# A gate's x*sigmoid(x) as one ScalarE function, and a visit's two exponentials as one instruction

## The chip, the core and the metric

The kernel runs on one core of one Trainium2 chip. A core has five engines that run side by side, each through its own list of instructions, in order: TensorE (PE in the rows, with its weight loads as PEld), VectorE (DVE), ScalarE (ACT), GpSimd (POOL) and SyncE (SP), which here only issues DMAs. They wait for one another through semaphores. TensorE writes its products to PSUM, which has eight banks of 128 x 512 numbers. The metric is the device time of one execution in microseconds (us).

## What is computed

Attention over 8 batches, 8 heads, 576 positions and 64 numbers per head, with a mask that leaves each position 32 earlier ones, next to each other for the first four heads and four apart for the last four; then a gated layer on the 4608 x 512 result.

```python
def _attn_ref(q, k, v):
    scores = scale * np.matmul(q, k.transpose(0, 1, 3, 2))
    ...
    scores = np.where(masks[None, :, :, :], scores, -1000000000.0)
    scores = scores - np.max(scores, axis=-1, keepdims=True)
    attn = np.exp(scores)
    attn = attn / (np.sum(attn, axis=-1, keepdims=True) + 1e-09)
    return np.matmul(attn, v).astype(np.float32)

def _moe_ref(x, w_gate, w_val, w_out):
    g = x @ w_gate
    silu = g * (1.0 / (1.0 + np.exp(-g)))
    val = x @ w_val
    return (silu * val @ w_out).astype(np.float32)
```

w_gate and w_val are 512 x 1536, w_out is 1536 x 512, all float32.

## The kernel before

Every float32 factor of the gated layer is split into a high and a low part, and a product is three matmuls (high by high, low by high, high by low).

The attention is cut into packs of tokens. The first four packs are done in an opening stage. Each later pack m has two **visits**, A and B, that are placed between the matmuls of the gated layer by the table `visit`: 31 packs are handled so (4 to 34). Visit A of a pack does, on TensorE, the result products of the pack before (L522) and its own scores (L459), both in the bank pair `two`; then VectorE normalizes the former (L530 to L532) and takes mask, maximum and difference of the latter (L477, or L472 for pack 4, then L479 and L480), and ScalarE takes the exponentials in `far_exps`. These are two instructions over the same 128 x 512 numbers, once to `s` (L492) and once in place to `e` (L487 in `exps`). Four DMAs (L497) then exchange quarters between the two, and VectorE transposes at visit B (L511).

The **plain stage** runs the gated layer on the first three chunks of 512 tokens, in 36 steps s (12 slices f of the 1536 columns for each chunk). A step is 12 matmuls into bank `bg` (gate, L587), 12 into `bv` (value, L587) and 12 output matmuls of the step before (L636). Each of `bg` and `bv` is one bank. So the gate matmuls of step s+1 wait until the readers of step s are done with `bg`: `act_tanh` on ScalarE, which writes t = tanh(g/2) to SBUF (L608), and `dve_u` on VectorE, which computes (t+1)*g from `bg` (L613). `dve_h` then multiplies by 0.5 and by `bv` (L618), and the result is split by ScalarE (L623) and GpSimd (L628).

During the first chunk the weights are still coming in as 64-bit integers. A unit u (half a slice f) is turned into its two parts by steps on three engines: ScalarE L253 and, for some units, L270; VectorE L273 and L283, or L280 alone; ScalarE L290 (high part); GpSimd L294 (low part). Units 0 and 1 are done in pieces, the rest as 128 x 768. Step s needs units 2s and 2s+1, and the conversion runs about one step ahead.

The **mixed stage** does the other three chunks (of 1024 tokens) with seven products of half-size blocks in place of eight. `keep` (L939, ScalarE) copies a bank that the next products go on adding to; `total` (L895, VectorE) adds bank and copy; `gated` applies tanh (L960) and the two VectorE steps (L962, L963) to these sums in SBUF; `h_split` splits the result (L924, L895).

The opening stage stands in an order written out by hand. After it a scheduler orders the instructions of each engine by its own estimates, kept by dependences and by the `behind(...)` marks. Tanh and Exp run from one table of ScalarE, which is loaded once at the start (L678).

Of the kernel before, what the change touches and what calls it, by code (L numbers as in the profile page):

```python
# [15 lines left out]
AF = mybir.ActivationFunctionType  # L16
ALU = mybir.AluOpType

P = 128
D = 64  # L20
# [121 lines left out]
def attention_moe(ctx, tc, qkb, vb, w, masks, ident, out):  # L142
# [201 lines left out]
    early, later = {}, {}  # L344
    for k, n in (("qk", QKB), ("v", NG * NH * (D + 1)), ("e", TP), ("pt", TP)):
        later[k] = Ring(n, o)
        o += n
# [96 lines left out]
    def scores(m, two, masked):  # L444
# [9 lines left out]
        for j in range(NH):  # L454
            for g in range(NG):
                q, k = BQ * (NH * g + j), FQN + pk(m).kcol[g, j] + o
                for h in range(2):
# [3 lines left out]
                                     stop=not masked or j == NH - 1, skip_group_check=True)  # L461

    def shift(m, two, pool, masked):

        mx, s, e = pool["bm"](2 * NH), pool["pt"](TP), pool["e"](TP)
        w = BK - 1 + masked
# [18 lines left out]
    def exps(m):  # L485
        e = st[m]["e"]
        last["e"] = nc.scalar.activation(out=e, in_=e, func=AF.Exp, scale=0.125)  # L487

    def far_exps(m):

        e, s = st[m]["e"], st[m]["s"]
        nc.scalar.activation(out=s, in_=e, func=AF.Exp, scale=0.125)  # L492
        exps(m)
        for g in range(0, NG, 2):
# [110 lines left out]

    def act_tanh(i):
        t = t_ring()
        last["t"] = nc.scalar.activation(out=t, in_=bank_g[:, :CH], func=AF.Tanh, scale=0.5)  # L608
        hst[i] = [t, None, None]

    def dve_u(i):
        t = hst[i][0]
        last["h"] = nc.vector.scalar_tensor_tensor(out=t, in0=t, scalar=1.0, in1=bank_g[:, :CH],  # L613
                                                   op0=ALU.add, op1=ALU.mult)

    def dve_h(i):
        t = hst[i][0]
        last["h"] = nc.vector.scalar_tensor_tensor(out=t, in0=t, scalar=0.5, in1=bank_v[:, :CH],  # L618
                                                   op0=ALU.mult, op1=ALU.mult)

# [333 lines left out]
    def gated(i, t):  # L954
# [4 lines left out]
        f = f_ring()  # L959
        nc.scalar.activation(out=f, in_=g, func=AF.Tanh, scale=0.5)  # L960
        v = total(t, 1, v_ring)
        nc.vector.scalar_tensor_tensor(out=f, in0=f, scalar=1.0, in1=g, op0=ALU.add, op1=ALU.mult)  # L962
        nc.vector.scalar_tensor_tensor(out=hq[a, b, i], in0=f, scalar=0.5, in1=v, op0=ALU.mult, op1=ALU.mult)  # L963
        if t == 6:
# [27 lines left out]
    for s in range(NS):  # L992
# [5 lines left out]
        else:  # L998
            gv_mm(ci, f, 0)
        act_tanh(s)  # L1000
        attend(3 * s)
        dve_u(s)
        late = visit.get(3 * s + 1, "B")[0] == "A"
# [139 lines left out]
```

## Time and profile before

| | |
|---|---|
| time, median of 3 runs | 891.49 us (890.86 to 892.4) |
| the profiled execution | 890.97 us, of which the span from first to last instruction is 889.2 us |
| TensorE busy | 879.5 us (99%) |
| VectorE busy | 675.8 us (76%), 1067 instructions |
| ScalarE busy | 380.4 us (43%), 615 instructions |
| GpSimd busy | 272.3 us (31%) |
| granted TensorE clock | 1.00 in every stretch |

A busy share is an average over stages. What the time depends on is which engine the others wait for in each stage, so the waits of TensorE are read beside it. Line numbers (L613) are those of the kernel before; the kernel after has the same places a few lines off, and where an instruction stream of it is shown its own line numbers stand.

### The profile page before, as it was taken

The page shows a single profiled execution, that of the slowest core. Times are in us where ns is not written, and L with a number is a line of the kernel's source. Part 1 is how long each engine was busy: PE and PEld are TensorE (multiplying, and loading weights), DVE is VectorE, ACT ScalarE, POOL GpSimd, SP SyncE. Part 2 cuts the span into 40 slices and gives each one's busy share as a digit, 9 for nine tenths or more (in the row PEclk, how much of TensorE's full clock was granted, in tenths as well). Part 3 has the DMA queues.
Part 4 walks back from the last instruction along what each step waited for, and adds up shares of the span by engine and source line. Part 5 has one row for each costly group of instructions (what it writes and reads, how often), then busy time and mean ns, then how long its engine had stood idle before and what let it go on. Part 6 is the DMA issues. An engine that isn't in the chain of part 4 may idle for free.

```text
span 889.2 us, 19625 instructions
## 1 busy us (share of the span) xinstructions
PE 879.5 (99%) x7954; PEld 719.1 (81%) x7954; DVE 675.8 (76%) x1067; ACT 380.4 (43%) x615; POOL 272.3 (31%) x313
## 2 busy tenths in 40 slices
PE   8999999999999999999999999999999999999998
PEld 5778888888888888888888888888888888888886
DVE  7876658997899993777699966787799755556963
ACT  6877533433332342333355533343455423334451
POOL 4967631211121222323333112333322113333310
PEclk9999999999999999999999999999999999999999
DMA  9975518768778775887777877887766776666672
GB/s 343 379 287 203 165 59 296 258 224 273 240 267 277 251 247 199 260 242 239 247 234 235 261 249 252 259 251 240 231 217 217 244 224 190 189 192 195 196 221 97
DMA packets 78698, 207.91 MB, mean 234 GB/s; under 512 B 9456, under 2 KB 28016, under 8 KB 78608
## 3 DMA queue, kind: packets, MB, share of 16 engines
q0 software_dynamic: 27520, 100.16, 36.8%
q1 hardware_dynamic: 41872, 70.33, 22.6%
q10 hardware_dynamic: 9216, 36.17, 11.7%
q8 instruction: 63, 1.03, 0.5%
q14 instruction: 27, 0.22, 0.1%
HBM read 159.96 MB, written 42.47 MB: 228 GB/s over the span
## 4 chain that ended last, share of the span: by engine, by line
PE 96%; DMA 2%; DVE 1%; ACT 0%; issue 0%; DVEq 0%; SPq 0%
PE bo L934 33%; PE bv L934 12%; PE bg L934 12%; PE bo L636 11%; PE bg L587 11%; PE bv L587 11%; PE two L522 3%; PE two L459 2%; DMA at_float<-qkb 1%; DMA at_int<-w 1%; ACT at_int L253 0%; DVE at_int L283 0%; DVE at_int L280 0%; DVE at_int L273 0%; ACT at_int L270 0%
## 5 line engine op out<-in xcount | busy, mean ns | idle before, releaser
L934 PE MATMUL bo<-at_float32r 128*128 128x512 f32 x1296 | 306.1, 390 | 0.0
L934 PEld LDWEIGHTS bo<-at_float32r 128*128 128x128 f32 x1296 | 242.5, 188 | 50.9
L861 POOL DMA_DIRECT2D at_float32r<-pieces x189 | 101.3, 536 | 351.0 <-PE bo L934 210.8
L895 DVE TENSOR_TENSOR at_float<-bo,at_float 128x512 f32<-128x512 f32 (+1 forms) x169 | 112.4, 679 | 66.7 <-PE bo L934 33.4
L895 DVE TENSOR_TENSOR at_float32r<-at_float,at_float32r 128x512 fp32r<-128x512 f32 (+1 forms) x147 | 112.2, 792 | 26.1 <-ACT at_float32r L924 19.5
L934 PE MATMUL bv<-at_float32r 128*128 128x512 f32 x486 | 128.2, 390 | 0.0
L934 PE MATMUL bg<-at_float32r 128*128 128x512 f32 x486 | 128.2, 390 | 0.0
L934 PEld LDWEIGHTS bg<-at_float32r 128*128 128x128 f32 x486 | 91.1, 188 | 19.0
L934 PEld LDWEIGHTS bv<-at_float32r 128*128 128x128 f32 x486 | 90.9, 188 | 19.1
L628 POOL TENSOR_TENSOR at_float32r<-at_float,at_float32r 128x512 fp32r<-128x512 f32 x36 | 51.5, 1431 | 172.8 <-PE bo L636 87.6
L636 PE MATMUL bo<-at_float32r,at_float32r 128*128 128x512 f32 x432 | 104.4, 390 | 0.0
L587 PE MATMUL bg<-at_float32r,at_float32r 128*128 128x512 f32 x420 | 101.9, 391 | 0.8 <-DVE at_float L613 0.8
L924 ACT CAST at_float32r<-at_float 128x512 fp32r<-128x512 f32 x126 | 75.4, 620 | 63.5 <-PE bv L934 16.3
L587 PE MATMUL bv<-at_float32r,at_float32r 128*128 128x512 f32 x420 | 101.7, 391 | 0.0
L636 PEld LDWEIGHTS bo<-at_float32r,at_float32r 128*128 128x128 f32 x432 | 80.7, 188 | 17.0
L587 PEld LDWEIGHTS bg<-at_float32r,at_float32r 128*128 128x128 f32 x420 | 78.3, 188 | 17.8 <-DVE at_float L613 1.2
L587 PEld LDWEIGHTS bv<-at_float32r,at_float32r 128*128 128x128 f32 x420 | 78.4, 188 | 16.6
L960 ACT ACTIVATE at_float<-at_float 128x512 f32<-128x512 f32 x72 | 45.4, 631 | 94.2 <-DVE at_float L895 94.2
L939 ACT COPY at_float<-bg 128x512 f32<-128x512 f32 x63 | 36.9, 586 | 87.8 <-PE bg L934 87.5
L895 POOL TENSOR_TENSOR at_float<-at_float,at_float 128x512 f32<-128x512 f32 x36 | 51.6, 1434 | 23.2 <-DVE at_float L963 13.0
L962 DVE SCALAR_TENSOR_TENSOR at_float<-at_float,at_float 128x512 f32<-128x512 f32 x72 | 49.4, 686 | 10.7 <-ACT at_float L960 10.1
L294 POOL TENSOR_TENSOR at_float32r<-at_int,at_float32r 128x768 fp32r<-128x768 f32 (+2 forms) x26 | 47.1, 1823 | 20.5 <-ACT at_float32r L290 20.5
(84 smaller groups left out, 856.3 us busy)
## 6 DMA issues: line engine op xcount, KB each, us to landing
at_float32r<-pieces POOLq DMA_DIRECT2D x189, 512.0 KB, 4.4
pieces<-at_float32r SPq DMA_DIRECT2D x126, 256.0 KB, 3.2
at_int<-w SPq DMA_DIRECT2D x24, 768.0 KB, 6.7
at_float<-vb ACTq DMA_DIRECT2D x31, 520.0 KB, 5.1
at_float<-qkb ACTq DMA_DIRECT2D x16, 640.0 KB, 6.6
out<-at_float SPq DMA_DIRECT2D x35, 256.0 KB, 4.0
at_float<-qkb ACTq DMA_DIRECT2D x15, 576.0 KB, 6.4
at_float<-at_float SPq DMA_DIRECT2D x128, 32.0 KB, 3.4
```

The lines of the kernel that those rows point to most:

```text
L294: nc.gpsimd.tensor_tensor(out=lo, in0=wst[u]["y"][:, a:b].bitcast(F32), in1=hi, op=ALU.subtract)
L522: nc.tensor.matmul(out=two[BQ * j:BQ * j + BQ, p, (D + 1) * x:(D + 1) * (x + 1)], lhsT=t[r, BQ * i:BQ * i + BQ], rhs=v[r, i, :], start=Tru ...
L587: last["g", which] = nc.tensor.matmul(out=bank.rearrange("p (n c) -> p n c", n=2), lhsT=wcol(f, o, low), rhs=x[l][j], start=n == 0, stop=n ...
L628: last["l"] = nc.gpsimd.tensor_tensor(out=hl, in0=hst[i][0], in1=hst[i][1], op=ALU.subtract)
L636: nc.tensor.matmul(out=bank_o[j][:, :CH], lhsT=wcol(f, 2 * DM + P * j, low), rhs=x, start=f == 0 and low == 0 and x is hh, stop=f == NF - ...
L861: nc.gpsimd.dma_start(out=taken[asked], in_=pieces[asked % NPIECE])
L895: x = engine.tensor_tensor(out=out, in0=a, in1=b, op=op)
L924: nc.scalar.copy(out=o[:, 0], in_=src)
L934: nc.tensor.matmul(out=bank, lhsT=w, rhs=x, start=first and n == 0 and t in FRESH, stop=last and n == len(ops) - 1, skip_group_check=True)
L939: nc.scalar.copy(out=kept[KEPT[t]][r], in_=banks[0][r][:, :CS])
L960: nc.scalar.activation(out=f, in_=g, func=AF.Tanh, scale=0.5)
L962: nc.vector.scalar_tensor_tensor(out=f, in0=f, scalar=1.0, in1=g, op0=ALU.add, op1=ALU.mult)
```

## The change

`act_silu` takes the place of `act_tanh`: ScalarE computes x*sigmoid(x) from `bg` by one function, and `dve_u` goes. `dve_h` becomes a plain product with `bv`. `gated` does the same in the mixed stage. So 36 + 72 VectorE instructions of 128 x 512 go. The tiles `e` and `s` of a visit become the two halves of one 128 x 1024 tile, and one instruction writes both halves, reading `e` twice by a broadcast.

```diff
-    for k, n in (("qk", QKB), ("v", NG * NH * (D + 1)), ("e", TP), ("pt", TP)):
+    for k, n in (("qk", QKB), ("v", NG * NH * (D + 1)), ("pt", TP), ("e", TP)):
...
+    def pair():
+        return at(later["pt"].starts[0], 2 * TP).rearrange("q (n c) -> q n c", n=2)
+
     def shift(m, two, pool, masked):
-        mx, s, e = pool["bm"](2 * NH), pool["pt"](TP), pool["e"](TP)
+        mx = pool["bm"](2 * NH)
+        s, e = [pair()[:, n] for n in range(2)]
...
     def far_exps(m):
         e, s = st[m]["e"], st[m]["s"]
-        nc.scalar.activation(out=s, in_=e, func=AF.Exp, scale=0.125)
-        exps(m)
+        last["e"] = nc.scalar.activation(out=pair(), in_=e.unsqueeze(1).broadcast_to([P, 2, TP]), func=AF.Exp, scale=0.125)
...
-    def act_tanh(i):
+    def act_silu(i):
         t = t_ring()
-        last["t"] = nc.scalar.activation(out=t, in_=bank_g[:, :CH], func=AF.Tanh, scale=0.5)
+        last["t"] = nc.scalar.activation(out=t, in_=bank_g[:, :CH], func=AF.Silu)
         hst[i] = [t, None, None]
-
-    def dve_u(i):
-        t = hst[i][0]
-        last["h"] = nc.vector.scalar_tensor_tensor(out=t, in0=t, scalar=1.0, in1=bank_g[:, :CH],
-                                                   op0=ALU.add, op1=ALU.mult)
 
     def dve_h(i):
         t = hst[i][0]
-        last["h"] = nc.vector.scalar_tensor_tensor(out=t, in0=t, scalar=0.5, in1=bank_v[:, :CH],
-                                                   op0=ALU.mult, op1=ALU.mult)
+        last["h"] = nc.vector.tensor_tensor(out=t, in0=t, in1=bank_v[:, :CH], op=ALU.mult)
...
         f = f_ring()
-        nc.scalar.activation(out=f, in_=g, func=AF.Tanh, scale=0.5)
+        nc.scalar.activation(out=f, in_=g, func=AF.Silu)
         v = total(t, 1, v_ring)
-        nc.vector.scalar_tensor_tensor(out=f, in0=f, scalar=1.0, in1=g, op0=ALU.add, op1=ALU.mult)
-        nc.vector.scalar_tensor_tensor(out=hq[a, b, i], in0=f, scalar=0.5, in1=v, op0=ALU.mult, op1=ALU.mult)
+        nc.vector.tensor_tensor(out=hq[a, b, i], in0=f, in1=v, op=ALU.mult)
```

The built programs differ in one thing that the diff does not say: Exp and Silu do not stand in one table. The kernel before has one ACT_TABLE_LOAD, the kernel after has 64: the one at the start, 31 ahead of exponentials and 32 ahead of Silu (18 in the plain stage, 14 in the mixed one). TensorE's order is the same but for one place, where the mixed stage begins.

**ScalarE, step 0 of the plain stage, before.** `at_776_int` are the buffers of units on their way to L290 (427 is unit 2, 345 unit 3, 409 unit 1 and then unit 4), `bg` the gate bank:

```order
L270 ACTIVATE at_1536_int_185<-at_1536_int_185 128x768
L290 CAST at_1536_float32r<-at_776_int_427 128x768
L608 ACTIVATE at_512_float_216<-bg 128x512
L290 CAST at_1536_float32r<-at_776_int_345 128x768
L253 ACTIVATE at_1536_int_187<-at_1536_int_187 128x768
L290 CAST at_1536_float32r<-at_776_int_409 128x512
L253 ACTIVATE at_1536_int_189<-at_1536_int_189 128x768
L623 CAST at_512_float32r<-at_512_float_216 128x512
```

And the same place after:

```order
L270 ACTIVATE at_1536_int_185<-at_1536_int_185 128x768
L290 CAST at_1536_float32r<-at_776_int_427 128x768
L611 ACT_TABLE_LOAD
L611 ACTIVATE at_512_float_216<-bg 128x512
L290 CAST at_1536_float32r<-at_776_int_345 128x768
L290 CAST at_1536_float32r<-at_776_int_409 128x512
L620 CAST at_512_float32r<-at_512_float_216 128x512
L253 ACTIVATE at_1536_int_187<-at_1536_int_187 128x768
```

A table load stands between unit 2's high part and the gate's function; two preparing steps have moved behind the split of the step's result.

**VectorE, the same place, before** (`at_1536_int_180`, 183 and 185 are the raw units 1, 2 and 3):

```order
L280 SCALAR_TENSOR_TENSOR at_776_int_409<-at_1536_int_180 128x256
L273 TENSOR_SCALAR at_776_int_427<-at_1536_int_183 128x3x256
L283 SCALAR_TENSOR_TENSOR at_776_int_427<-at_1536_int_183,at_776_int_427 128x3x256
L280 SCALAR_TENSOR_TENSOR at_776_int_345<-at_1536_int_185 128x3x256
L613 SCALAR_TENSOR_TENSOR at_512_float_216<-at_512_float_216,bg 128x512
L280 SCALAR_TENSOR_TENSOR at_776_int_409<-at_1536_int_180 128x2x256
L618 SCALAR_TENSOR_TENSOR at_512_float_216<-at_512_float_216,bv 128x512
```

And after:

```order
L280 SCALAR_TENSOR_TENSOR at_776_int_409<-at_1536_int_180 128x256
L280 SCALAR_TENSOR_TENSOR at_776_int_409<-at_1536_int_180 128x2x256
L273 TENSOR_SCALAR at_776_int_427<-at_1536_int_183 128x3x256
L283 SCALAR_TENSOR_TENSOR at_776_int_427<-at_1536_int_183,at_776_int_427 128x3x256
L280 SCALAR_TENSOR_TENSOR at_776_int_345<-at_1536_int_185 128x3x256
L616 TENSOR_TENSOR at_512_float_216<-at_512_float_216,bv 128x512
```

`dve_u` is gone, and the second piece of unit 1 (128 x 512) has moved ahead of unit 2's two steps.

**ScalarE, the first visit A (pack 4, between steps 2 and 3), before:**

```order
L290 CAST at_1536_float32r<-at_776_int_345 128x768
L362 DMA at_1280_float_191<-qkb 128x1152
L492 ACTIVATE at_512_float_349<-at_512_float_318 128x512
L608 ACTIVATE at_512_float_239<-bg 128x512
L487 ACTIVATE at_512_float_318<-at_512_float_318 128x512
```

And after:

```order
L290 CAST at_1536_float32r<-at_776_int_345 128x768
L362 DMA at_1280_float_191<-qkb 128x1152
L290 CAST at_1536_float32r<-at_776_int_409 128x768
L496 ACT_TABLE_LOAD
L496 ACTIVATE at_1024_float_706<-at_1024_float_706 128x1024
L611 ACT_TABLE_LOAD
L611 ACTIVATE at_512_float_239<-bg 128x512
```

The gate's function stood between the two exponentials; now it stands behind the one exponential and a second table load, and one more conversion (which waits for VectorE's L273 and L283 of its unit, now ahead of the visit's first step there) stands ahead of both.

## Rows read from the trace of the kernel before

**Rows 1.** The page's first part: busy time, share of the span, instructions.

```profile
PE 879.5 (99%) x7954; PEld 719.1 (81%) x7954; DVE 675.8 (76%) x1067; ACT 380.4 (43%) x615; POOL 272.3 (31%) x313
```

**Rows 2.** Windows: stretch, its us, each engine's busy us, PEclk, DMA, GB/s.

```profile
0.00:20.00 20.00, 15.86 (x261) 9.54 (x265) 15.11 (x28) 12.06 (x19) 7.77 (x15) 1.00 0.91 335
20.00:45.00 25.00, 23.46 (x130) 18.12 (x130) 20.70 (x25) 20.97 (x32) 22.80 (x16) 1.00 0.98 381
...
790.00:889.00 99.00, 95.50 (x422) 78.74 (x420) 62.69 (x95) 38.32 (x65) 23.52 (x35) 1.00 0.57 179
```

**Rows 3.** TensorE's waits: who for whom, us in total, times, longest.

```profile
PE bg L587 <- DVE at_float L613: 0.8, 1, 0.8
```

**Rows 4.** Timeline, step 0, all engines: start, us, engine, instruction [idle before].

```profile
24.21 0.58 DVE L280 SCALAR_TENSOR_TENSOR at_int<-at_int 128x256 int32<-128x256 int32 x1
...
24.82 0.95 DVE L273 TENSOR_SCALAR at_int<-at_int 128x768 int32<-128x768 int32 x1
...
25.81 1.68 DVE L283 SCALAR_TENSOR_TENSOR at_int<-at_int,at_int 128x768 int32<-128x768 int32 x1
...
27.43 1.47 DVE L280 SCALAR_TENSOR_TENSOR at_int<-at_int 128x768 int32<-128x768 int32 x1
27.52 0.83 ACT L290 CAST at_float32r<-at_int 128x768 fp32r<-128x768 f32 x1 [0.17 <-DVE at_int L283]
...
28.26 0.59 ACT L608 ACTIVATE at_float<-bg 128x512 f32<-128x512 f32 x1
...
28.88 0.69 DVE L613 SCALAR_TENSOR_TENSOR at_float<-at_float,bg 128x512 f32<-128x512 f32 x1
...
29.49 1.57 DVE L280 SCALAR_TENSOR_TENSOR at_int<-at_int 128x512 int32<-128x512 int32 x1
...
29.62 3.02 PE L587 MATMUL bg<-at_float32r,at_float32r 128*128 128x512 f32 x12 [0.76 <-DVE at_float L613]
```

**Rows 5.** Timeline of ScalarE: the one table load and what follows it.

```profile
1.18 1.28 ACT L678 ACT_TABLE_LOAD   x1 [1.18 <-PEq L1135]
2.48 0.20 ACT L678 ACTIVATE at_float<-at_float 128x2 f32<-128x2 f32 x1
```

**Rows 6.** Groups by shape: count | busy us, mean ns | idle before.

```profile
L900 ACT CAST at_float32r<-at_float 128x1024 fp32r<-128x1024 f32 x21 | 22.1, 1052 | 24.6 <-PE bo L934 13.6 <-DVE at_float L895 8.0 <-DVE at_float L555 2.5
...
L492 ACT ACTIVATE at_float<-at_float 128x512 f32<-128x512 f32 x32 | 20.2, 632 | 43.7 <-DVE at_float L480 43.6
...
L283 DVE SCALAR_TENSOR_TENSOR at_int<-at_int,at_int 128x768 int32<-128x768 int32 x10 | 10.5, 1045 | 0.3
...
L280 DVE SCALAR_TENSOR_TENSOR at_int<-at_int 128x512 int32<-128x512 int32 x2 | 2.3, 1130 | 0.0
```

**Rows 7.** Timeline at the first visit A, steps 3 and 4.

```profile
49.64 0.92 DVE L480 TENSOR_TENSOR at_float<-at_float,at_float 128x512 f32<-128x512 f32 x1
...
52.35 0.94 DVE L273 TENSOR_SCALAR at_int<-at_int 128x768 int32<-128x768 int32 x1
...
53.33 0.96 DVE L283 SCALAR_TENSOR_TENSOR at_int<-at_int,at_int 128x768 int32<-128x768 int32 x1
...
55.29 2.88 PE L587 MATMUL bg<-at_float32r,at_float32r 128*128 128x512 f32 x12
```

**Rows 8.** Timeline of steps 17 and 18 (chunk 1).

```profile
178.92 0.59 ACT L608 ACTIVATE at_float<-bg 128x512 f32<-128x512 f32 x1
179.66 0.68 DVE L613 SCALAR_TENSOR_TENSOR at_float<-at_float,bg 128x512 f32<-128x512 f32 x1
...
181.32 1.98 PE L587 MATMUL bg<-at_float32r,at_float32r 128*128 128x512 f32 x8
```

**Rows 9.** ScalarE's waits, the longest group (the mixed stage's tanh).

```profile
ACT at_float L960 <- DVE at_float L895: 94.2, 64, 4.2
```

More of the change, by code (lines that the diff above doesn't have):

```diff
@@ L999, in attention_moe @@
             gv_mm(ci, f, 0)
-        act_tanh(s)
+        act_silu(s)
         attend(3 * s)
-        dve_u(s)
         late = visit.get(3 * s + 1, "B")[0] == "A"
```

## The prediction

> **What bounds the kernel now.** I read the page's busy times first, then the windows over the whole span, then TensorE's waits, and then the timeline at the places where the change touches what TensorE waits for. By busy time TensorE is the bound: 879.5 us of a span of 889.2, against 675.8 on VectorE and 380.4 on ScalarE [rows 1]. So 9.7 us are all that any other engine can cost it now. The windows say where: 4.1 us in the first 20 us, 1.5 in the next 25 and 3.5 in the last 99, at the end of the kernel [rows 2]; in between it is busy without a gap, at a granted clock of 1.00. Of the waits of TensorE one alone lies on something that the change touches: the gate bank's second group, which waits once, for 0.8 us, for VectorE's L613 [rows 3], 0.76 us in the timeline of step 0 [rows 4]. That sets the terms: work taken off VectorE, however much, can return at most 0.8 us, and work put on ScalarE costs something only where a reader of `bg` comes so late that TensorE waits. The sum is therefore made at the handoffs of `bg` and not from totals.
>
> **VectorE, removed.** 36 + 72 instructions at about 0.69 us, the time of the L613 at step 0 [rows 4], are some 74 us: VectorE goes to about 602 us. This is off the path, and worth nothing but for the 0.76 us above.
>
> **The two exponentials.** Two instructions at 0.632 us (1.26) become one of 128 x 1024. No such exponential is in the trace; the conversion of that shape on ScalarE takes 1.052 us [rows 6], and between that and 1.26 I take 1.05. The gain, 0.2 us times 31, is off the path: ScalarE stands idle for 43.7 us in all ahead of L492, waiting for VectorE's L480 [rows 6]. What the fusion changes is the order: the gate's function no longer fits between the two.
>
> **The table loads, added.** Exp and Tanh shared a table, Exp and Silu do not: 64 loads in place of one. The one in the trace takes 1.28 us, with the next instruction 20 ns behind it [rows 5], so 63 x 1.28 = 81 us more on ScalarE. With 31 x 0.2 us less for the exponentials it goes from 380 to some 454 us, half the span: no bound by throughput. What counts is where a load stands between `bg` being full and its reader's end.
>
> **Step 0.** Before, the gate's function starts at 28.26, when unit 2's conversion lets ScalarE go, L613 follows at 28.88 and TensorE at 29.62 [rows 4]. After, L613 is gone, but two things come in: the second piece of unit 1 (L280, 128 x 512) now stands on VectorE ahead of unit 2's L273 and L283, and a load stands between unit 2's conversion (L290) and the gate's function. From the end of L280's first piece, and the start of its next neighbour at 24.82, I add 1.57 (L280), 0.95 (L273), 1.05 (L283), 0.83 (L290), 1.28 (load) and 0.59 (the function, at Tanh's price) = 6.27, and six handoffs of some 0.03 each: 31.29. TensorE started at 29.62, so it is **1.7 us** later, and the 0.76 us of waiting grow to 2.4. The terms have bounds. The two L280 of that shape average 1.130, so the other took 0.69 [rows 6]; with that the sum is 0.8 us. L283 took 1.68 here, when GpSimd and ScalarE were at work beside it, but 1.045 in the mean of ten [rows 6]; with 1.68 it is 2.3. I take 1.57 because it is measured in this very stretch, and the mean for L283 since the operation that lay beside it moves. Behind step 0 the conversions of later units slip by the one L280 and the load, 1.1 to 1.35 us by VectorE's and ScalarE's order, which is less than TensorE's own 1.7: no further stall comes of them.
>
> **The first visit.** Now L480 ends at 50.56, and TensorE begins the next gate group at 55.29 [rows 7], without a wait. After, L480 ends between 52.26 (all merely shifted by 1.7) and 54.16 (the L273 and L283 of a unit, 0.94 and 0.96 [rows 7], put ahead of it too). Behind it come the exponential 1.05, the load 1.28, the function 0.59 and a handoff 0.05: 55.2 to 57.1. TensorE needs the bank at 55.29 + 1.7 = 57.0. So 0 to 0.1 us; I take nothing. The load for the exponential itself stands ahead of its wait for L480 and lies in that wait.
>
> **Later visits.** In steps without a visit nothing is added, and the old path loses L613. With a visit, the load (1.28) takes the place of L613 (0.68) and its handoff. The tightest later place is step 17: the function starts at 178.92, L613 ends at 180.34, TensorE starts at 181.32 [rows 8], 0.98 us of room. After: 178.92 + 1.28 + 0.59 + 0.05 = 180.84, so 0.48 us of room are left, and the load is hidden by TensorE's own matmuls into `bv` and `bo`. If that cover were gone it would cost the difference, at worst 1.28 per visit.
>
> **The mixed stage.** Silu there reads a sum in SBUF, not a bank. It waited for VectorE's totals for 94.2 us over 64 times [rows 9], 1.5 us each, so 14 loads of 1.28 disappear in that wait, and exponentials' loads in the wait of L492.
>
> **The sum.** 0 (VectorE) + 0 (exponentials) + 1.7 (step 0) + 0 (visits) + 0 (mixed stage) = 1.7 us. The profiled execution took 890.97 us, which gives 892.7; the median of the runs is 0.5 above it, 891.49, and on that scale the forecast is **893.2 us**. That is 0.19%, just at the 0.2% (1.8 us) that a measurement of this kernel can tell from no change.
>
> By the Trainium skill (ScalarE: Activation LUTs, "Table sets: the hidden batching unit") calls of functions should be batched by table set, with exp and tanh in one set; this change alternates two sets where there was one. The trace agrees on one half, one load in the kernel before [rows 5], and TensorE's 99% says why the rule need not cost much here.
>
> **Rivals.**
> *The load is hidden at step 0 as well.* If L280's piece takes its 0.69 and the load runs while ScalarE would wait for L283, the load drops out of the path and the second gate group starts at 31.29 - 0.88 - 1.28 = 29.1, at or before the 29.62 of now. Against it: the load stands behind L290 in the order, so it can't begin before L283 is done. Between 0.76 us gained and 0.4 lost: 890.7 to 891.9.
>
> *A switch in mid-stream costs more than the row.* The one load in the trace ran on an idle engine [rows 5]; behind a running instruction it may have to wait until the engine is empty. Suppose twice the 1.28. Step 0 pays 1.28 more (3.0), the first visit 0.1, and step 17 lacks 1.28 - 0.48 = 0.8: +3.8, or 895.3. It decides from a price of 1.28 + 0.48 on. The same page of the skill, in "What ACT_TABLE_LOAD costs", gives 1283 ns for the load and about 1380 ns for a drain ahead of it, 2.66 us a switch; step 0 would be +3.1 by that in place of +1.7. The trace shows the first figure, and no run so far the second.
>
> *Visits stall TensorE: the slower side.* ScalarE works in order, and the gate's function now stands behind the exponential and so behind VectorE's mask, maximum and difference. If at step 17 and its like the exponential ends 0.48 us later than Tanh began before, TensorE waits in the plain stage. At six of the 18 visits by 0.5 us each this is 3.0 on top of 1.7: 896.2. For it: the order shown at the first visit, where the function has moved from between the exponentials to behind them. Against it: room of 0.98 us at the tightest place, and VectorE has 74 us less to do, so L480 comes no later.
>
> *Faster.* To gain over 1.8 us TensorE's idle 9.7 us would have to shrink by work that touches it; 0.76 us are touched, the rest lies in the opening (4.1) and at the end (3.5) [rows 2], where nothing has moved.
>
> **How the numbers follow.** Forecast (0.8 to 2.3 at step 0, nothing elsewhere): 0.47, half of it past the 1.8 us, 0.24 slower and 0.23 same. Load hidden: 0.19, same. Dearer switch: 0.10, slower. Visits stall: 0.20, slower. Faster: 0.04. So 0.04 faster, 0.42 same, 0.54 slower. The range goes from 891.2, the lower part of the hidden case left out, to 896.3, which takes in both dearer cases at their worked prices and leaves out what of the visits' case is worse.
>
> **What would show it.** 64 loads at 1.28 us, each followed at once by its function. The second gate group at about 31.3 with a wait of 2.4 us for ScalarE's Silu; TensorE's busy time unchanged near 879.5, its clock 1.00; VectorE near 602, ScalarE near 454. No other wait of `bg` for ScalarE beyond 0.1 us. It is wrong if gate groups wait at several visits, if the gap between the instruction ahead of a load and the one behind it is well over 1.3 us, or if step 0's L280 and L283 run at other times than taken.

## The result: 7.2 us slower

| | time, median | ratio to before, 95% interval |
|---|---|---|
| the kernel before, on the same chip | 891.83 us (4 runs) | |
| the kernel after | 899.05 us (898.05 to 900.19, 4 runs) | 1.0082 (1.0065 to 1.0100) |

The forecast was 893.2 us, with a range up to 896.3. The direction was right, the size was not: 7.2 us in place of 1.7, and outside the range. The profiled execution of the kernel after has a span of 896.3 us, 7.1 more than the 889.2 of before, so its trace holds the whole loss.

The page's busy times, which answer to [rows 1]:

```profile
PE 881.0 (98%) x7954; PEld 718.8 (80%) x7954; DVE 623.2 (70%) x959; ACT 454.7 (51%) x646; POOL 274.8 (31%) x313
```

ScalarE came out as foreseen, at 454.7 us, and TensorE is still the bound: 881.0 of 896.3 us. Its idle time went from 9.7 us to 15.3; the other 1.5 us of the 7.1 stand in its busy time, in part because a gate group behind a wait takes 3.01 or 3.02 us in place of 2.88 (the rows below). The windows of TensorE's idle time say where. First the kernel before, in two stretches that [rows 2] leave out, then the kernel after in the same stretches and the one behind them (stretch, us, busy us of PE, PEld, DVE, ACT and POOL, PEclk, DMA, GB/s):

```profile
45.00:80.00 35.00, 34.71 (x419) 28.23 (x420) 25.24 (x33) 26.51 (x38) 23.52 (x14) 1.00 0.75 268
80.00:120.00 40.00, 40.00 (x478) 32.91 (x465) 27.24 (x42) 23.34 (x34) 24.60 (x15) 1.00 0.45 154
```

```profile
45.00:80.00 35.00, 33.28 (x327) 26.82 (x326) 22.46 (x27) 27.07 (x34) 21.48 (x13) 1.00 0.65 242
80.00:120.00 40.00, 36.48 (x480) 29.14 (x481) 27.76 (x33) 28.35 (x36) 26.86 (x16) 1.00 0.43 145
120.00:160.00 40.00, 40.00 (x482) 32.95 (x470) 26.68 (x46) 17.23 (x24) 10.78 (x8) 1.00 0.52 180
```

TensorE lacks 0.3 us and nothing there before, 1.7 and 3.5 us after; from 120 us on it is full again. (In the opening and at the end the idle time is as before, within some 0.3 us.) So the loss lies in the first chunk, while the weights are being converted. TensorE's waits, the group that answers to [rows 3], and the four places in its timeline (start, us, instruction, idle before):

```profile
PE bg L590 <- ACT at_float L611: 6.2, 4, 1.9
```

```profile
30.55 3.02 PE L590 MATMUL bg<-at_float32r,at_float32r 128*128 128x512 f32 x12 [1.45 <-ACT at_float L611]
...
57.65 3.02 PE L590 MATMUL bg<-at_float32r,at_float32r 128*128 128x512 f32 x12 [1.27 <-ACT at_float L611]
...
96.31 3.01 PE L590 MATMUL bg<-at_float32r,at_float32r 128*128 128x512 f32 x12 [1.92 <-ACT at_float L611]
...
116.24 3.01 PE L590 MATMUL bg<-at_float32r,at_float32r 128*128 128x512 f32 x12 [1.60 <-ACT at_float L611]
```

One wait of 0.8 us for VectorE has become four for ScalarE's function, 6.2 us in all. Set against the same matmuls of the kernel before, TensorE comes later by these steps:

| place | before | after | added |
|---|---|---|---|
| gate group of step 1 | 29.62 | 30.55 | 0.93, of which 0.23 ahead of this wait |
| gate group of step 4 (visit of pack 4) | 55.29 | 57.65 | 1.43 |
| results at the next visit | 61.18 | 63.84 | 0.30 |
| gate group of step 8 (visit of pack 6) | 91.55 | 96.31 | 2.10 |
| gate group of step 10 (visit of pack 7) | 109.50 | 116.24 | 1.98 |
| all that follows | | | 0.33 |
| end of the span | 889.2 | 896.3 | 7.07 |

### The profile page after: what moved, and what is told of

It reads as the page before. It is cut to its first block, busy times and chain, and to the rows that moved or that the text cites. A ratio compares the mean times of both kernels' runs of the same rounds, so it can differ in the third digit from the quotient of the medians.

```text
span 896.3 us, 19581 instructions
## 1 busy us (share of the span) xinstructions
PE 881.0 (98%) x7954; PEld 718.8 (80%) x7954; DVE 623.2 (70%) x959; ACT 454.7 (51%) x646; POOL 274.8 (31%) x313
## 4 chain that ended last, share of the span: by engine, by line
PE 91%; DVE 3%; DMA 3%; ACT 2%; issue 1%; POOL 0%; DVEq 0%; SPq 0%; ACTq 0%
PE bo L931 33%; PE bv L931 12%; PE bg L931 12%; PE bo L633 10%; PE bg L590 9%; PE bv L590 9%; PE two L525 3%; PE two L459 2%; DMA at_int<-w 2%; DVE at_int L280 1%; ACT L611 1%; DMA pieces<-at_float32r 1%; DVE at_int L283 1%; DVE at_float L375 0%; ACT at_int L253 0%
## 5 line engine op out<-in xcount | busy, mean ns | idle before, releaser
L892 DVE TENSOR_TENSOR at_float32r<-at_float,at_float32r 128x512 fp32r<-128x512 f32 (+1 forms) x147 | 114.1, 808 | 35.4 <-ACT at_float32r L921 28.5
L959 DVE TENSOR_TENSOR at_float<-at_float,at_float 128x512 f32<-128x512 f32 x72 | 49.3, 686 | 15.9 <-ACT at_float L957 13.3
```

The source lines that it names most:

```text
L892: x = engine.tensor_tensor(out=out, in0=a, in1=b, op=op)
L959: nc.vector.tensor_tensor(out=hq[a, b, i], in0=f, in1=v, op=ALU.mult)
```

## What happens at a visit now

At the visit of pack 6 the kernel before has these rows on TensorE, VectorE and ScalarE:

```profile
83.39 2.88 PE L587 MATMUL bg<-at_float32r,at_float32r 128*128 128x512 f32 x12
```

```profile
83.62 0.69 DVE L480 TENSOR_TENSOR at_float<-at_float,at_float 128x512 f32<-128x512 f32 x1
...
87.61 0.95 DVE L273 TENSOR_SCALAR at_int<-at_int 128x768 int32<-128x768 int32 x1
```

```profile
84.34 0.63 ACT L492 ACTIVATE at_float<-at_float 128x512 f32<-128x512 f32 x1 [0.17 <-DVE at_float L480]
...
86.31 0.60 ACT L608 ACTIVATE at_float<-bg 128x512 f32<-128x512 f32 x1 [0.19 <-PE bg L587]
```

The bank of this step is full at 86.27. The visit's last vector step ends at 84.31, two microseconds earlier, so both exponentials are out of the way and Tanh starts at once. The conversion (L273) comes later. The kernel after, same visit, TensorE, VectorE and then ScalarE:

```profile
86.07 2.88 PE L590 MATMUL bg<-at_float32r,at_float32r 128*128 128x512 f32 x12
```

```profile
87.23 0.96 DVE L280 SCALAR_TENSOR_TENSOR at_int<-at_int 128x768 int32<-128x768 int32 x1 [1.76 <-ACT at_int L270]
...
89.09 1.08 DVE L283 SCALAR_TENSOR_TENSOR at_int<-at_int,at_int 128x768 int32<-128x768 int32 x1
...
92.56 0.69 DVE L484 TENSOR_TENSOR at_float<-at_float,at_float 128x512 f32<-128x512 f32 x1
```

```profile
93.29 1.06 ACT L496 ACTIVATE at_float<-at_float 128x1024 f32<-128x1024 f32 x1 [2.92 <-DVE at_float L484]
94.36 1.28 ACT L611 ACT_TABLE_LOAD   x1
95.66 0.60 ACT L611 ACTIVATE at_float<-bg 128x512 f32<-128x512 f32 x1
```

The bank is full at 88.95. But conversion steps of two units (L280 of one, L273 and L283 of the next), the first of which waits 1.76 us for ScalarE's L270, now stand just ahead of the visit's vector steps. (Before, that L280 had started at 80.28, and the other unit's two steps stood behind the visit.) The last of the vector steps (L484) ends at 93.25, 4.3 us behind the full bank in place of 2.0 ahead of it. Then ScalarE adds the exponential (1.06), the load (1.28) and the function (0.60). TensorE's groups in `bv` and `bo` cover 5.4 us of this and it waits for the other 1.9.

At the visit of pack 7 it is ScalarE where a conversion has come ahead. VectorE's last step of the visit, and ScalarE ahead of the function:

```profile
106.42 1.50 DVE L484 TENSOR_TENSOR at_float<-at_float,at_float 128x512 f32<-128x512 f32 x1
```

```profile
112.92 0.84 ACT L290 CAST at_float32r<-at_int 128x768 fp32r<-128x768 f32 x1 [1.53 <-DVE at_int L283]
...
114.30 1.28 ACT L611 ACT_TABLE_LOAD   x1
```

L484 ends at 107.92, still 1.3 us ahead of the full bank (109.20; 3.2 us ahead before). But the high parts of 21 units of 128 x 768 now stand ahead of this function on ScalarE, in place of 20, and the last of them waits for its unit's L283 on VectorE until 112.92.

So two things meet: an order in which conversions come first, so that the vector steps or the function itself come late, and a load behind them. The first was in no term of the prediction for these visits. What follows separates them.

## Experiments

A theory of **loads**: each load ahead of the gate's function costs its own 1.28 us. A theory of **order**: the conversions moved ahead, mostly of the visits' vector steps, and only there do the loads find no room. To hold an order, these lines were added; ORDER lists each engine's instructions by their names, and the edges set the order of issue alone. TensorE was left to the scheduler.

```diff
+def pin(tc):
+    traced = {i.name: i for i in tc.nc.cur_bb.bb.instructions}
+    for names in ORDER.values():
+        ...
+        for a, b in zip(names, names[1:]):
+            tc.add_manual_dep(traced[b], a, mybir.DependencyInfo(
+                mybir.DependencyClass.NoSync, mybir.DependencyReason.DATA), reason="pin")
```

| kernel | loads | time | ratio to before, 95% interval |
|---|---|---|---|
| after's order, no loads | 1 | 893.97 | 1.0025 (1.0016 to 1.0035) |
| before's work and order, with loads | 66 | 906.87 | 1.0169 (1.0153 to 1.0186) |
| after's work in before's order | 64 | 894.98 | 1.0039 (1.0024 to 1.0054) |
| one exponential only | 1 | 892.43 | 1.0007 (0.9998 to 1.0017) |
| old order, then new | 64 | 892.82 | 1.0012 (1.0002 to 1.0021) |
| the same, table loaded early | 64 | 892.73 | 1.0006 (0.9997 to 1.0014) |
| Silu only | 82 | 904.84 | 1.0144 (1.0130 to 1.0158) |
| Silu in the mixed stage only | 28 | 892.60 | 1.0008 (0.9999 to 1.0017) |
| after, mark on the visit | 64 | 893.09 | 1.0012 (1.0003 to 1.0021) |
| the same, table loaded early | 64 | 892.66 | 1.0014 (1.0005 to 1.0023) |
| before, one mark looser | 1 | 895.92 | 1.0046 (1.0032 to 1.0059) |

The kernel before had medians of 891.73 to 891.99 beside these. A ratio is an estimate of its own and not quite that of the two medians.

### The order of after without its loads

```diff
-        last["t"] = nc.scalar.activation(out=t, in_=bank_g[:, :CH], func=AF.Silu)
+        last["t"] = nc.scalar.activation(out=t, in_=bank_g[:, :CH], func=AF.Tanh)
...
-        nc.scalar.activation(out=f, in_=g, func=AF.Silu)
+        nc.scalar.activation(out=f, in_=g, func=AF.Tanh)
```

> The kernel after with Tanh written where Silu stands (so the gate is not computed), and with every instruction of ScalarE, VectorE, GpSimd and SyncE held to the order of the kernel after: the same order, one table load in place of 64. Two theories. Loads: each load ahead of the gate's function costs by its own 1.28 us. Order: in the first chunk the visits' vector steps have moved behind weight conversions, so the exponential, and the gate's function behind it, end after the bank has been full for long, loads or not. Loads: the four waits for the gate's function (1.45, 1.27, 1.92, 1.60 us) shrink by 1.28 or 2.56 each, to 0, 0, 0.6 and 0.3, and the time falls from 899.1 to 893.8 or less. Order: the waits at the third and fourth place stay above 1 us each, TensorE's waits for the gate's function are 2.5 us or more in all, and the time is 895.5 or more.

893.97 us, close to the 893.8 of the theory of loads: the loads take 5.1 of the 7.2 us with them, and 2.2 remain with one load in the program. (TensorE, which was not held, differs in one place: three output matmuls have moved ahead of a visit at 62 us.) TensorE's waits:

```profile
PE two L525 <- DVE at_float L514: 1.4, 1, 1.4
PE bg L590 <- ACT at_float L611: 1.2, 2, 0.7
```

The waits for the gate's function shrink to two of 0.7 and 0.5 us, near the 0.9 in all of the theory of loads. But the late vector steps find a second way: late exponentials mean a late exchange by DMA, a late transposition on VectorE, and results that wait for it. VectorE's row, and TensorE's:

```profile
95.94 0.71 DVE L514 STREAM_TRANSPOSE at_float<-at_float 128x512 f32<-128x512 f32 x1 [2.96 <-DMA at_float<-at_float]
```

```profile
96.70 0.80 PE L525 MATMUL two<-at_float,at_float 64*32 64x65 f32 x60 [1.37 <-DVE at_float L514]
```

So the order costs by itself, though not by the way I had expected, and neither theory has all of it.

### The loads in the order of before

```diff
-        last["t"] = nc.scalar.activation(out=t, in_=bank_g[:, :CH], func=AF.Tanh, scale=0.5)
+        last["t"] = nc.scalar.activation(out=t, in_=bank_g[:, :CH], func=AF.Silu)
```

(and the same in `gated`)

> The kernel before with Silu written where Tanh stands and all else kept, both VectorE steps and both exponentials too (so the gate is not computed), held to the order of the kernel before: 66 or more table loads in the old order. Order: in the old order the gate bank has 2.9 to 3.9 us of room at the visits of the first chunk, and the loads fit; left are step 0 (1.3 us) and step 17 (0.3 us, since 0.98 of room meets 1.28): 893.4. Loads: stalls at the visits of the first chunk of over 1 us each, as in the kernel after: 896 or more.

906.87 us, far beyond either number, so this one does not tell the theories apart. With both VectorE steps kept, a load is added to every path and nothing taken from it: gate groups wait at step 1 (2.17 us), step 18 (1.49), and two later places (0.22 and 1.67), output groups in the mixed stage for 2.8 us. No gate group waits at a visit of the first chunk, which is what the theory of order says. Two things disturb the comparison: the scheduler moved the matmuls of two visits on TensorE, and after the wait at step 1 TensorE ran at half its clock:

```profile
31.00:34.00 3.00, 2.64 (x6) 2.15 (x7) 1.51 (x3) 3.00 (x6) 2.62 (x2) 0.50 0.65 224
```

0.50 of full speed is 1.2 GHz in place of 2.4, and the gate group took 4.40 us there in place of 3.02. The same happened once more at 311 us, behind waits of 1.67 and 1.32 us, and cost as much again. In all the profiled span is 15.8 us longer than that of before: 8.4 us of that are added idle time of TensorE, some 2.8 the low clock, and the rest was not traced.

### The work of after in the order of before

The lines of `pin`, with before's order.

> The kernel after with its work unchanged (Silu, 64 loads, one exponential for a visit), held to the order that the kernel before has on ScalarE, VectorE, GpSimd and SyncE. Order: only step 0 waits longer, for the load without VectorE's second step, some 0.6 us; no visit stalls; 892.4. Loads: the waits at three visits of the first chunk stay at 1 us or more each; 896 or more.

894.98 us: between the two. In the first chunk the theory of order is right: with 64 loads in the program no visit stalls, and TensorE waits once, 1.4 us, at step 1.

```profile
PE bo L931 <- DVE at_float L892: 2.5, 2, 1.3
...
PE bg L590 <- ACT at_float L611: 1.4, 1, 1.4
```

The first line is new, two waits in the mixed stage that neither kernel has. VectorE at the first of them, just ahead of the totals that TensorE waits for:

```profile
385.02 0.71 DVE L514 STREAM_TRANSPOSE at_float<-at_float 128x512 f32<-128x512 f32 x1 [4.72 <-DMA at_float<-at_float]
385.66 1.85 DVE L892 TENSOR_TENSOR at_float<-bo,at_float 128x512 f32<-128x512 f32 x3
```

The totals stand behind a transposition that waits 4.72 us for the visit's exchange by DMA. That exchange is issued at 378.61 us, behind a load and the exponential, where the kernel before issues it at 376.87; TensorE itself is only 0.7 us later by then. The scheduler's new order does not have this pair of waits.

### The old order in the plain stage, the new one behind it

The lines of `pin`; ORDER is that of before as far as 352 us, and that of after from there.

> The kernel after with its work unchanged (64 loads), its four engines held to the order of the kernel before up to the end of the plain stage (352 us) and to the order of the kernel after from there on. If the cost of the change lies in the order of the first chunk together with the loads, and the 2.5 us that output groups waited for VectorE's totals in the experiment with the old order throughout lie in its mixed stage, both are gone: only step 0 waits, 1.4 us in place of 0.8, and the time is 892.6. If the loads cost by themselves wherever they stand, 895 or more.

892.82 us, as the theory of order has it: with 64 loads all but some 1 us of the loss is gone, and TensorE waits for the function at step 1 alone. So the loads at the visits are hidden when the visits' steps come first. The 11 runs fall apart, though: seven at 891.6 to 892.8 us with a mean clock of 0.999 or 1.000, four at 894.3 to 894.9 with 0.996 or 0.997. The profiled one is of the four. TensorE's row at step 1, and a window behind it of this kernel and of the kernel after:

```profile
30.72 4.61 PE L590 MATMUL bg<-at_float32r,at_float32r 128*128 128x512 f32 x12 [1.45 <-ACT at_float L611]
```

```profile
31.00:34.00 3.00, 3.00 (x9) 2.34 (x9) 1.03 (x2) 3.00 (x6) 2.54 (x2) 0.54 0.72 267
```

```profile
31.00:34.00 3.00, 3.00 (x15) 2.47 (x14) 0.22 (x1) 3.00 (x6) 2.70 (x2) 1.00 1.01 413
```

Both waited 1.45 us ahead of this group. In one execution the granted clock fell to 0.54 over the next 3 us and 12 matmuls took 4.61 us in place of 3.02, in the other it stayed at 1.00. A wait of this length was thus paid a second time in one of these executions, and not in the other.

### The table loaded early

```diff
+    nc.scalar.activation(out=some, in_=some, func=AF.Silu)
+
     for s in range(NS):
```

(held in ScalarE's order behind the opening's last exponential)

> As the experiment with the old order and then the new one, and besides a Silu of 128 x 2 numbers directly behind the last exponential of the opening (near 17 us, where ScalarE waits for a DMA), so that step 0's load is done there and not between the full gate bank and its function. Loads on the path: TensorE's wait at step 0 falls from 1.4 us to under 0.3, and the time by 1.0 or more: 891.6. Rival: ScalarE is full from 17 us to 30 us, the load only moves everything behind it, and the time stays at 892.6.

The mechanism is as expected, and the time hardly moves: 892.73 us, where 891.6 was expected. ScalarE at the opening and at step 0, and TensorE:

```profile
16.50 1.28 ACT L988 ACT_TABLE_LOAD   x1
...
28.34 0.83 ACT L290 CAST at_float32r<-at_int 128x768 fp32r<-128x768 f32 x1 [0.36 <-DVE at_int L283]
29.08 0.59 ACT L611 ACTIVATE at_float<-bg 128x512 f32<-128x512 f32 x1
```

```profile
29.73 3.06 PE L590 MATMUL bg<-at_float32r,at_float32r 128*128 128x512 f32 x12
```

The wait of 1.4 us is gone, and TensorE starts at 29.73 in place of 30.72. Nor is there an execution at a low clock: all 11 have 0.998 or more, and the slowest took 893.41 us in place of 894.9. That the wait brought those on is not shown by it, since the version with the mark, further down, keeps the wait and has none under 0.998 in 11 either. But its median is no better than that of the quick seven of the experiment before, though TensorE is 1 us earlier at step 1. What gave the 1 us back is open: against the kernel before, the profiled execution is 0.1 us late at step 1 and loses 0.4 and 0.8 us more at two places of the mixed stage, and no trace of the quick seven was taken to set beside it.

### Each part alone

One exponential only, the change's second part put into the kernel before:

```diff
...
-        nc.scalar.activation(out=s, in_=e, func=AF.Exp, scale=0.125)
-        exps(m)
+        last["e"] = nc.scalar.activation(out=pair(), in_=e.unsqueeze(1).broadcast_to([P, 2, TP]), func=AF.Exp, scale=0.125)
```

> The kernel before with the second part of the change alone: one exponential instruction for a visit, Tanh and both VectorE steps kept, one load, the order left to the scheduler. Both theories: 891.8, no wait of TensorE beyond the 0.8 at step 0 by over 0.3 us. A rival: the fused instruction alone makes the scheduler put the gate's function behind late exponentials; then waits of 1 us or more at visits of the first chunk, 893.5 or more.

892.43 us: the second part of the change costs nothing that can be told. It takes 34.0 us on ScalarE for 32 instructions, 1061 ns each. Silu only, the kernel after with the same lines turned round:

```diff
...
-        last["e"] = nc.scalar.activation(out=pair(), in_=e.unsqueeze(1).broadcast_to([P, 2, TP]), func=AF.Exp, scale=0.125)
+        nc.scalar.activation(out=s, in_=e, func=AF.Exp, scale=0.125)
+        exps(m)
```

> The first part of the change alone: Silu in place of Tanh and a VectorE step, a visit's two exponentials kept apart, order left to the scheduler; the program has 82 loads. Loads in the scheduler's own order: the more of them, the dearer, at 5 us for the 63 of the kernel after some 6.5 for 81, and with the order's 2.2 together 900.5. Rival: fusing the exponentials is what let the gate's function slip behind them; then the waits at the first chunk's visits are under 1 us each and the time is 896 or less.

904.84 us, dearer than both guesses. The groups of loads show one reason why the fused instruction matters: ten times the function stands between the two exponentials, and the second needs a load of its own.

```profile
L487 ACT ACT_TABLE_LOAD x10 | 12.8, 1283 | 0.2
```

```profile
PE two L522 <- DVE at_float L511: 6.9, 4, 3.0
PE bg L587 <- ACT at_float L608: 3.3, 3, 1.4
```

Its waits are those of the order again, 6.9 us for late transpositions among them. So the two parts of the change belong together, and the second saves 5.8 us of what the first costs. Silu in the mixed stage only, on top of the one exponential:

```diff
-        nc.scalar.activation(out=f, in_=g, func=AF.Tanh, scale=0.5)
+        nc.scalar.activation(out=f, in_=g, func=AF.Silu)
...
-        nc.vector.scalar_tensor_tensor(out=f, in0=f, scalar=1.0, in1=g, op0=ALU.add, op1=ALU.mult)
-        nc.vector.scalar_tensor_tensor(out=hq[a, b, i], in0=f, scalar=0.5, in1=v, op0=ALU.mult, op1=ALU.mult)
+        nc.vector.tensor_tensor(out=hq[a, b, i], in0=f, in1=v, op=ALU.mult)
```

> One exponential for a visit, Silu in the mixed stage alone, Tanh and the VectorE step in the plain stage: 28 loads, none ahead of a reader of the gate bank. The loads hide in ScalarE's waits for totals: 892.4, as with one exponential alone, and no wait of TensorE over 0.3 us in the mixed stage. Rival: the loads delay the bank copies or the totals there, 1 us or more at two places or more: 894.5.

892.60 us, as with one exponential alone: 27 more loads, and in the mixed stage one wait of TensorE for VectorE's totals, of 0.3 us.

### Why the order changed

All these pins left one question: what made the scheduler put the conversions first? The code marks the conversions of a step with `behind("h", "t", "x")`: on VectorE they are issued behind the last instruction noted as `h`. `dve_u` noted itself there. It ran behind Tanh of the same step, and so mostly behind the visit. With `dve_u` gone, `h` is `dve_h` of the step before, and the conversions may go first. Two experiments, one from each side, with the scheduler free otherwise:

```diff
-        with behind("h", "t", "x"):
+        with behind("h", "t", "x", "s"):
```

(twice, in the kernel after; `s` is the visit's L484)

> The kernel after, and the two marks behind(h, t, x) around the weight conversions also name the visit's last vector step (s, the L484 of the kernel after); the scheduler is free otherwise; 64 loads. Theory on the order: dve_u, which the change took out, was also what these marks named on VectorE (last h), so without it the conversions were held only behind dve_h of the step before and went ahead of the visits' vector steps. With a mark on the visit they go back behind it: no wait for the gate's function at a visit, 1.4 us at step 0 alone, 893.0. If the loads by themselves were the cause, the time stays above 897.

```diff
     def dve_u(i):
         t = hst[i][0]
-        last["h"] = nc.vector.scalar_tensor_tensor(out=t, in0=t, scalar=1.0, in1=bank_g[:, :CH],
+        nc.vector.scalar_tensor_tensor(out=t, in0=t, scalar=1.0, in1=bank_g[:, :CH],
```

(in the kernel before)

> The kernel before with all its work (Tanh, both VectorE steps, two exponentials, one load), and one name less: dve_u no longer sets last h, so the marks name dve_h of the step before, as they do in the kernel after. Theory on the order: the conversions go ahead of the visits' vector steps here too, and TensorE waits for late transpositions (L511) and the gate's function in the first chunk, 1 us or more in all; 893.5, by the 2.2 us that the order of the kernel after cost without its loads. If the mark is not what moved them, 891.9.

The first gives 893.09 us where 893.0 was expected: 6 us of the 7.2 come back by a name in two lines, with all 64 loads in place. The visit of pack 6 on VectorE, ScalarE and TensorE:

```profile
84.36 0.69 DVE L484 TENSOR_TENSOR at_float<-at_float,at_float 128x512 f32<-128x512 f32 x1
84.97 2.06 DVE L280 SCALAR_TENSOR_TENSOR at_int<-at_int 128x768 int32<-128x768 int32 x1
```

```profile
87.92 1.28 ACT L611 ACT_TABLE_LOAD   x1
89.21 0.60 ACT L611 ACTIVATE at_float<-bg 128x512 f32<-128x512 f32 x1
```

```profile
92.78 2.88 PE L590 MATMUL bg<-at_float32r,at_float32r 128*128 128x512 f32 x12
```

The vector steps end at 85.05, ahead of the full bank, Silu ends at 89.8, and TensorE starts at 92.78 without a wait: 3 us of room, with the load in it. At pack 7 ScalarE again has 20 units' high parts ahead of the function, and 3.0 us of room. The second gives 895.92 us, more than the 893.5 expected: no load and no operation is changed, one name is taken out of the marks, and the kernel before loses 4.0 us. VectorE at the same visit:

```profile
87.17 1.39 DVE L283 SCALAR_TENSOR_TENSOR at_int<-at_int,at_int 128x768 int32<-128x768 int32 x1
...
90.96 0.69 DVE L480 TENSOR_TENSOR at_float<-at_float,at_float 128x512 f32<-128x512 f32 x1
```

The conversion stands ahead of the visit, as in the kernel after, and TensorE waits 1.31 us for the next gate group; at the visit of pack 5 it waits 2.42 us, until 63.56, for results whose transposition ends at 63.45. So the mark is what moved the order. By these runs the new order without the loads costs 2.2 us, the loads without the new order 1.1, and the other 3.9 of the 7.2 us come only when both meet. Last, both repairs together, the mark and the early table:

```diff
+    with behind("e"):
+        nc.scalar.activation(out=some, in_=some, func=AF.Silu)
+
     for s in range(NS):
...
-        with behind("h", "t", "x"):
+        with behind("h", "t", "x", "s"):
```

> As the experiment with the mark on the visit, and a Silu of 128 x 2 numbers directly behind the opening's last exponential, so that step 0's load is done near 17 us. No wait of TensorE for the gate's function over 0.2 us anywhere, 892.2: within 0.1% of the kernel before, with 64 loads in the program. If the marks do not repair the order, waits of 1 us or more at two visits remain and the time is 896 or more.

892.66 us, and no wait for the gate's function. The early load did not bring TensorE forward here: its row for step 1 stands at 31.03, as without it (31.08): ScalarE's work in the opening stands behind the load, and matmuls of step 0 that wait for it came up to 2.1 us later than in the kernel before. That is the rival of the pinned experiment, right in this order and wrong in that one. No version came out faster than the kernel before; with TensorE at 99% there was nothing to win, as the prediction said.

## The prediction, point by point

**What bounds the kernel: right.** TensorE stayed the bound, and the 52.6 us that VectorE lost (675.8 to 623.2) were worth nothing. I expected 74 us there. The 108 instructions went, but other steps grew longer: L283 takes 1404 ns in the mean after, 1045 before [rows 6], L280 of 128 x 768 takes 1346 in place of 1124, and a split in the plain stage (L823, now L820, 36 times) 884 in place of 712, some 12 us together. Besides, neighbouring rows of VectorE overlap by up to 0.1 us, so that an instruction that goes gives back a little less than its row.

**The loads' size: right.** There are 64, and all groups have a mean of 1283 ns, on an idle engine or a busy one:

```profile
L496 ACT ACT_TABLE_LOAD x31 | 39.8, 1283 | 9.2 <-PE bo L633 4.4 <-DMA pieces<-at_float32r 1.9 <-PE two L459 1.4
...
L611 ACT ACT_TABLE_LOAD x18 | 23.1, 1283 | 0.3
...
L957 ACT ACT_TABLE_LOAD x14 | 18.0, 1283 | 3.4 <-DVE at_float L892 3.2
```

ScalarE was to reach 454 us and reached 454.7; the exponential was to take 1.05 us and took 1.06. The rival of a dearer switch is out: at the visit of pack 6 the exponential ends at 94.35, the load starts at 94.36 and the function 20 ns behind its end. The Trainium skill (ScalarE: Activation LUTs, "What ACT_TABLE_LOAD costs") adds about 1380 ns of drain to each switch, without saying on which side of the load; no row here shows it, ahead of a load or behind one, and the measurement decides.

**Step 0: right mechanism, too large.** VectorE and then ScalarE there:

```profile
24.14 1.61 DVE L280 SCALAR_TENSOR_TENSOR at_int<-at_int 128x256 int32<-128x256 int32 x2
...
26.65 1.08 DVE L283 SCALAR_TENSOR_TENSOR at_int<-at_int,at_int 128x768 int32<-128x768 int32 x1
```

```profile
28.61 1.28 ACT L611 ACT_TABLE_LOAD   x1
29.90 0.60 ACT L611 ACTIVATE at_float<-bg 128x512 f32<-128x512 f32 x1
```

The chain is the one of the sum, and TensorE started at 30.55 in place of 31.29. The term that was mis-sized is L280's 1.57: its two pieces together took 1.61, of which 1.1 are the larger one's, halfway between the bounds 0.69 and 1.57. That piece also began 0.2 us earlier than I had taken. L283 took 1.08, as taken from the mean. What the step itself added is 0.7 us, where 1.7 stood in the sum. The rival of a hidden load is out: it starts at 28.61, right behind L290. (Two sums of the prediction are off by a rounding: step 0's terms give 31.27 and not 31.29, those of the dearer switch 3.9 and not 3.8.)

**The first visit: right chain, both ends off.** I had the function's end between 55.2 and 57.1 and TensorE's need at 57.0. The function ended at 57.60, since L283 ahead of the visit took 2.03 us in place of 0.96, and the need came at 56.2, since step 0 had cost less. Both errors went the same way and made 1.4 us out of 0.

**Later visits: this is the step that failed.** I took the rooms of the kernel before, found the smallest (step 17, 0.98 us), and put the load into it, with ScalarE's function starting where it started before. Step 17 indeed does not wait. The visits that do, of packs 6 and 7, had 3.8 and 3.4 us of room before (L613 ended at 87.70 and 106.07, TensorE came at 91.55 and 109.50), and I passed over them; but at pack 6 the vector steps had moved by 6.3 us against TensorE, and at pack 7 one more conversion stood ahead of the function on ScalarE. The order at the first visit showed it (a unit's L273 and L283 ahead of the visit's first step), I entered it there as a shift of 1.9 us, and did not ask what had held those steps back until now, or whether it was gone everywhere.

**The rival of stalling visits: right mechanism, too small and in another place.** It had the function behind the exponential and late vector steps, and 3.0 us at places like step 17 with a chance of 0.20. It was 5.8 us between 55 and 117 us, by the steps of the table above, and 4.8 of them are waits for the function. What I held against it, that VectorE has less to do and L480 comes no later, is the wrong sentence: fewer instructions on an engine do not make a given one earlier when the order changes with them.

**The mixed stage: right.** No wait of TensorE there in the kernel after; the 14 loads lie in ScalarE's waits for totals, and the experiment with Silu in this stage alone shows the same by its time.

## What to carry to other kernels

An instruction that is removed may also be the anchor that an order hangs on: look for every mark, semaphore or priority that names it before costing its removal at nothing. When the built order is at hand, compare it at every place of a kind and not at the one with the smallest room before, since the rooms themselves move with the order. In this kernel a function from another table was cheap where its load fell into a wait of ScalarE (64 loads for 1.1 us with the mark on the visit), and dear behind work that came late (5.1 us in the order of after).

## What I had not expected of the hardware

In two profiled executions a wait of TensorE cost more than its length: after 1.45 us in the experiment with the old order and then the new one, and after 2.17 us in the one with loads in before's order, the granted clock stood at 0.50 to 0.54 (1.2 GHz) in the 3 us window that followed, and the gate group took 4.4 to 4.6 us in place of 3.0. After a wait of the same 1.45 us in the kernel after it stayed at 1.00, and so it did in three more versions (the order of before throughout, Silu only, the mark on the visit). What sets these executions apart was not found. L280 and L283 on VectorE took between 0.92 and 2.06 us for one shape (128 x 768) in the two kernels: none of them took over 0.96 us with no GpSimd step beside it, and those beside one took 0.94 to 2.06. L273 of the same shape took 0.91 to 0.95 us beside a GpSimd step as well. Why some of the others stay short was not tried.
